# Top-k attention with a routed expert layer: scatters of routed rows right behind the search in the first 66 slots, block pieces from slot 12 of a batch

## The chip, the cores and the metric

The kernel runs on one core of one Trainium2 chip. The metric is the device time of one execution in microseconds (us), and lower is better. Five engines of the core appear in the profile: PE (matrix multiply; PEld is its weight load), DVE (vector), ACT (scalar, activation functions), POOL (GpSimd) and SP (issues DMAs here). Each engine runs its own instructions in the order in which they were written to it, and waits for others through semaphores.

## The reference: what is computed

There are two stages. The first is attention that keeps, for each query, the scores that reach the 32nd largest:

```
scores = scale * (q @ k.T)                  # 8 batches, 8 heads, 576 x 576, head size 64
kth    = 32nd largest of each row
p      = exp(where(scores >= kth, scores, -1e9) - rowmax)
attn   = (p / (sum(p) + 1e-9)) @ v
x      = attn, reshaped to 4608 tokens x 512
```

The second sends each token to one of eight experts:

```
logits = x @ w_gate                         # 4608 x 8
e      = argmax(logits);  gate = softmax(logits)[e]
y      = gate * (relu(x @ w1[e]) @ w2[e])   # w1: 512 x 1024, w2: 1024 x 512
```

All data are 32-bit floats.

## The kernel before, in words

**Slots.** The attention is cut into 144 slots, 18 for each of the 8 batches (`work`, `per_batch`). A slot handles two tiles of 128 queries by 576 keys. The function `loop` (from L1233) writes the instructions slot by slot. In the text slot 25 is the 26th; "slot 2.7" is slot 7 of batch 2, which is slot 43.

**One slot.** In the order in which they are written:

- DVE folds the scores of the *next* slot into halves: larger (`h`, L320) and smaller (`l`, L321). The search of this slot follows (`search`, L358). It works on the larger quarter (`few`) and on short lists of what was set aside (`lists`, L354), and takes eight maxima at a time (MAX8, L379), four times for each tile, with the found ones struck out in between (L390).
- Inside the search `fold_on` (L324) folds `h` of the next slot once more: the larger of each pair into `few` (L327, DVE), the smaller into `hl`. `hl` is made in one of two ways. *Aside*: POOL computes it as a sum of integers less the larger one (L332 and L333). Otherwise DVE takes the minimum (L335). In the aside form `fold_on` stands after the second pass of the search; otherwise it stands before the fourth (after the second too in a "heavy" slot).
- ACT turns the found threshold into `low` (L401) and applies a steep ReLU to the scores (`depths`, L417). POOL subtracts the result from the scores (`less`, L426, twice per slot), so that all below the threshold vanishes in the exponential. POOL also makes `nbias` (L385) and keeps doubts (L407).
- ACT copies later scores out of PSUM (L311). PE transposes the weights of the slot before (L445, L461), does pieces of expert work, and ACT takes the exponential (L434). PE multiplies the scores of the slot four ahead (L304).

**Aside or not.** L1258 to L1260: `loose` holds for slots 1 to 65 (`QUIET = 66`). `soon`, which selects the aside form, holds in a loose slot if `k.crowded` is false. `k.crowded` is set by any scatter, by any store of a finished block and by `rows`. In a slot in which attention rows are scaled by POOL (L519 to L533), the slot is `heavy` and takes the DVE form.

**The end of a batch.** Some slots after a batch's last tile, `ending` (L1111) computes its routing. It is a generator that stops at named places (`yield "small"`, `yield "pool"`); `at_place(name)` in the loop lets it go on. Small DVE operations of it, here called ticks, are handed out one at a time between passes three and four of later searches (`tick`, L339): the choice of the expert (L545 to L558), the places of the tokens (L581 to L590), for the first batch `filled_up` (L696 to L706), and the table of blocks (`table`, L644 to L689). The rows go to `x_rows` in DRAM by five indirect DMAs that POOL issues (`scatter`, L601), one per slot, and only after the fifth are the next blocks' rows and weights loaded (`ahead`, through SP).

**Expert work.** A block is 128 rows of one expert, cut into 16 pieces for PE (eight of the first product, L979, and eight of the second, L996), with ACT evacuating (L870, L984, L1005) and POOL issuing the indirect store (L888). A rate, set anew in slot 13 of each batch (`FIRST`, L1016 and L1286), says how many pieces a slot takes. After the loop the remaining blocks run on PE alone. POOL's order is not written out by hand: what `in_turn` marks keeps its order, and a DMA is only told to stand after the instruction in `k.last_pool` (L606).

Of the kernel before, what the change touches and what calls it, by code (L numbers as in the profile page):

```python
# [12 lines left out]
ALU = mybir.AluOpType  # L13
# [31 lines left out]
def kernel(  # L45
# [47 lines left out]
    nc = tc.nc  # L93
# [40 lines left out]
    k = SimpleNamespace()  # L134
# [122 lines left out]
    def in_turn(put):  # L257

        if not k.exact:
            tc.keep_in_program_order(put)  # L260
        return put
# [62 lines left out]
    def fold_on(f, aside_too=False):  # L324

        f.few = k.att.tile([P, 2, LW], F32, name="few", bufs=3)
        nc.vector.tensor_tensor(f.few[:, :, 0:QF], f.h[:, :, 0:QF], f.h[:, :, QF:HF], op=ALU.max)  # L327
        hl = k.att.tile([P, 2, QF], I32, name="hl", bufs=1)
        f.hl, f.aside = hl[:, :, :].bitcast(F32), aside_too
        if aside_too:  # L330
            one, other, more = (a.bitcast(I32) for a in (f.h[:, :, 0:QF], f.h[:, :, QF:HF], f.few[:, :, 0:QF]))
            in_turn(nc.gpsimd.tensor_tensor(hl, one, other, op=ALU.add))  # L332
            in_turn(nc.gpsimd.tensor_tensor(hl, hl, more, op=ALU.subtract))  # L333
        else:
            nc.vector.tensor_tensor(f.hl, f.h[:, :, 0:QF], f.h[:, :, QF:HF], op=ALU.min)  # L335

# [76 lines left out]
    def depths(s, low):  # L413

        w = k.att.tile([P, 2, S], F32, name="w", bufs=1 if k.exact else 3)
        for m in range(2):
            nc.scalar.activation(  # L417
                w[:, m, :], s[:, m, :, :].rearrange("p j k -> p (j k)"), AF.Relu,
                scale=-STEEP, bias=low[:, m:m + 1],
            )  # L420
        return w
# [591 lines left out]
            evacuate()  # L1013

    PIECES = 2 * FT
    FIRST = 13  # L1016
    ARRIVED = 13
    AHEAD = 3
    QUIET = 66
# [4 lines left out]
    with fast:  # L1024
# [8 lines left out]
        per_batch = len(work) // B  # L1033
        x_of, lg_of = {}, {}
        waiting, loaded, coming, spare, scatters, stores = [], [], [], [], [], []
# [3 lines left out]
        def level(b):  # L1039

            have, sums = left / PIECES, []
            for n, new in enumerate(new_of[b:] + [0], 1):
                sums.append(have / n)
                have += new
            sums[-1] = (have - KEEP / PIECES) / (len(sums) - 1 + (per_batch - FIRST) / per_batch)
            return min(sums)
# [4 lines left out]
        def ahead():  # L1051
            while waiting and len(loaded) < 2:
                expert, piece = waiting.pop(0)
                if isinstance(piece, SimpleNamespace):
                    rows_in = piece
                elif isinstance(piece, list):
                    rows_in = load_half(load_rows(SimpleNamespace(), piece[0]), *piece[1:])
                elif isinstance(piece, tuple):
                    rows_in = load_rows(SimpleNamespace(), *piece, full=True)
                else:  # L1060
                    rows_in = load_rows(SimpleNamespace(), piece)
                loaded.append(load_weights(rows_in, expert))
                loaded[-1].at = clock
# [36 lines left out]
        def scatter(n):  # L1100
            nonlocal left
            for _ in range(min(n, len(scatters))):
                k.crowded = True
                scatters.pop(0)()
            if not scatters and coming:
                waiting.extend(coming)
                left += len(coming) * PIECES
                coming.clear()
                ahead()

        def ending(b, u):  # L1111

            nonlocal left
            n = unit[b * U + u]
            if u == 0:
                x_of[b] = k.xp.tile([P, KC, XW], F32, name="x")
                in_turn(token_ids(x_of[b][:, :, Dm + 1].bitcast(I32), b))
                lg_of[b] = k.small.tile([P, KC, E], F32, name="lg")
            x, lg = x_of[b], lg_of[b]
            out_steps = outputs(n, x)  # L1120
            yield "products"
            next(out_steps)
            yield "relu"
            next(out_steps)
            if u % 2 == 0:
                yield "relu"
            div = divisors(n)
            next(div)
            aside.append(div)
            yield "products"  # L1130
            next(out_steps)
            if b * U + u + 2 < len(units):
                load_values(unit[b * U + u + 2])
            yield "relu"
            next(out_steps)
            yield "products"
            next(out_steps)
            yield "relu"
            next(out_steps, None)
            yield "rows"  # L1140
            through(div)
            logits(n, lg)
            rows(n, x)
            if u < U - 1:
                return
            yield "small"
            r = choice(lg)
            aside.append(r.steps)
            yield "weights"
            yield "turn"  # L1150
            through(r.steps)
            nc.scalar.activation(lg, lg, AF.Exp)
            yield "products"
            ranks(r)
            yield "small"
            steps = places(r, x)
            aside.append(steps)
            yield "relu"
            nc.scalar.copy(run, r.run)
            if b:  # L1160
                nc.scalar.activation(blocks, r.run, AF.Copy, scale=1.0 / P, bias=UNDER)
            yield "pool"
            through(steps)
            scatters.extend(scattering(r, x))
            if b == 0:
                steps = filled_up()
                aside.append(steps)
                yield "weights"
                yield "pool"
                through(steps)  # L1170
            if b == B - 1:
                scatter(KC)
                slot_i = k.small.tile([1, 2, NSLOT], I32, name="slot_i")
                half, full, brief = counted()
                through(table(slot_i, SURE, False, half))
                nc.vector.tensor_scalar_add(done, done, -WHOLE)
                firsts = [(slot_i[0:1, 0, j:j + 1], slot_i[0:1, 1, j:j + 1]) for j in range(SURE)]
                ready = load_rows(SimpleNamespace(), firsts[0][1], True)
            new = LAST - SURE if b == B - 1 else new_of[b]
            if new:  # L1180
                if b == B - 1:
                    slot_i = slot_last
                    steps = end_table(slot_i, slot_long, new, half, full, brief)
                else:
                    slot_i = k.small.tile([1, 2, NSLOT], I32, name="slot_i")
                    steps = table(slot_i, new, False)
                aside.append(steps)
                for _ in range(3 if b < B - 1 else 2):
                    yield "weights"
                    yield "pool"  # L1190
                through(steps)
                coming.extend((slot_i[0:1, 0, j:j + 1], slot_i[0:1, 1, j:j + 1]) for j in range(new))
            if b == B - 1:
                spare.extend(coming[PLAIN:])
                del coming[PLAIN:]
                longs = [[slot_long[0:1, i, j:j + 1] for i in range(3)] for j in range(LONGS)]
                spare.extend((expert, half) for expert, half, _ in longs[HALVES:])
                coming[0:0] = [
                    (expert, [full, half, ST if j >= BRIEF else FEW])
                    for j, (expert, half, full) in enumerate(longs[:HALVES])  # L1200
                ]
                assert len(loaded) == 2
                fill_up()
                coming[0:0] = [(firsts[0][0], ready)] + [(expert, (piece,)) for expert, piece in firsts[1:]]
                scatter(0)
# [3 lines left out]
        def at_place(name):  # L1209
            for end in list(late):  # L1210
                if end[1] == name:
                    end[1] = next(end[0], None)
                    if end[1] is None:
                        late.remove(end)
# [18 lines left out]
        def loop():  # L1233
# [16 lines left out]
            for i, (b, g) in enumerate(work):  # L1250
# [7 lines left out]
                loose = 0 < i < QUIET  # L1258
# [14 lines left out]
                low, nbias, doubts = search(tiles, s_of[i], f_of.pop(i), then, soon, behind, beside)  # L1273
                k.crowded, k.heavy = held, False
                at_place("small")
                w_of[i] = depths(s_of[i], low)
                less(s_of.pop(i), w_of[i])
                doubts()
# [2 lines left out]
                    at_place("relu")  # L1281
                    at_place("rows")
                put_stores()
                scatter(1)
                at = i % per_batch
                if at == FIRST and b:  # L1286
                    rate = level(b) * PIECES / (U * NT)
# [70 lines left out]
    with ExitStack() as outer:  # L1358
        either = nc.values_load(rare_i[0:1, 0:1], min_val=0, max_val=P + 1)  # L1359
        outer.enter_context(tc.If(either > 0))  # L1360
        with ExitStack() as st:
            open_pools(st, True)
            more = nc.values_load(rest_i[0:1, 0:1], min_val=0, max_val=LAST + E)
# [110 lines left out]
```

## Time and profile before

| | |
|---|---|
| time, median of 3 runs | 1282.63 us (1281.47 to 1285.32) |
| time of the profiled execution | 1284.61 us |
| its span | 1283.0 us |
| PE busy | 1176.1 us, 92% of the span |
| DVE busy | 1058.8 us, 83% |
| ACT busy | 933.3 us, 73% |
| POOL busy | 732.0 us, 57% |

Busy times are unions of the instructions' records, so that overlapping records count once. A record of DVE includes time in which the instruction stands in the engine and can't go on. In the stretch of the slots, DVE shows no gaps: what it loses stands inside its records, and shows as a record that is longer than others of the same form. Slot lengths in the text are from the end of the last MAX8 of one slot's search to that of the next one's.

### The profile page before, as it was taken

The numbers are of one execution on the slowest core, as the hardware profiler recorded it, in microseconds if no ns is written. First come the engines' busy times: TensorE is split into PE (matmuls) and PEld (weight loads), VectorE is DVE, ScalarE is ACT, GpSimd is POOL, SyncE is SP. The second block draws the span as 40 slices with busy tenths as digits, with TensorE's granted clock in tenths as the row PEclk, the third lists the DMA queues.
The fourth block names the chain that finished last, engine by engine and source line by source line (L and its number), as shares of the span: only waits on it lengthen the run. The fifth ranks groups of instructions, "written<-read, shape, count | busy, mean of one in ns | idle before, by whom it ended". The sixth has DMA issues, their size and how long they took to land. (4 is left out here: it accounts for less than half of the span.)

```text
span 1283.0 us, 24461 instructions
## 1 busy us (share of the span) xinstructions
PE 1176.1 (92%) x7574; PEld 823.6 (64%) x7574; DVE 1058.8 (83%) x4608; ACT 933.3 (73%) x2136; POOL 732.0 (57%) x884
## 2 busy tenths in 40 slices
PE   6767767898899999999999999999999999999998
PEld 3444444665566566667666666666666667789975
DVE  8999999999999999999999999999999965000000
ACT  4888887988799888888788888888888872112121
POOL 4777777786678665658555855676557743101010
PEclk9888788999899999999999999999999999999999
DMA  5001113741474147533946464547555548996582
GB/s 153 31 30 31 31 39 126 263 157 39 146 251 162 39 150 283 182 135 98 332 142 218 163 224 153 189 146 264 178 178 202 172 149 285 353 358 235 215 301 83
DMA packets 98701, 220.81 MB, mean 172 GB/s; under 512 B 5309, under 2 KB 26301, under 8 KB 98560
## 3 DMA queue, kind: packets, MB, share of 16 engines
q1 hardware_dynamic: 91360, 198.87, 44.5%
q0 software_dynamic: 6384, 19.97, 4.2%
q8 instruction: 61, 1.00, 0.3%
q14 instruction: 80, 0.66, 0.2%
q10 hardware_dynamic: 816, 0.31, 0.1%
HBM read 195.75 MB, written 24.04 MB: 171 GB/s over the span
## 5 line engine op out<-in xcount | busy, mean ns | idle before, releaser
L426 POOL TENSOR_TENSOR w<-s,w 128x576 f32<-128x576 f32 x288 | 409.2, 1441 | 317.5 <-ACT w L417 317.4
L979 PE MATMUL ph<-xTs,w 128*128 128x128 f32 x2112 | 263.0, 278 | 2.6 <-ACT xTs L870 2.6
L979 PEld LDWEIGHTS ph<-xTs,w 128*128 128x128 f32 x2112 | 251.3, 194 | 21.1 <-issue 17.6
L996 PE MATMUL py<-w,hT 128*128 128x512 f32 x528 | 248.7, 600 | 1.9 <-ACT hT L984 1.6
L434 ACT ACTIVATE w<-w,nbias 128x576 f32<-128x576 f32 x288 | 223.0, 785 | 2.3 <-POOL w L426 1.4
L445 PE MATMUL wTm<-turn,w 128*128 128x128 f32 x1152 | 173.9, 291 | 52.7 <-ACT oT L484 29.1
L417 ACT ACTIVATE w<-s,low 128x576 f32<-128x576 f32 x288 | 207.7, 768 | 4.7
L304 PE MATMUL sc<-qkb 64*128 64x288 f32 (+1 forms) x1280 | 200.7, 465 | 7.8 <-DMA qkb<-in_qk_dram 4.0
L445 PEld LDWEIGHTS wTm<-turn,w 128*128 128x128 f32 x1152 | 135.1, 148 | 111.6 <-ACT oT L484 35.5
L311 ACT COPY s<-sc 128x576 f32<-128x576 f32 x288 | 168.0, 634 | 11.9 <-PE sc L304 11.8
L379 DVE MAX8 tops<-scr 128x8 f32<-128x168 f32 x576 | 169.5, 328 | 0.0
L452 ACT COPY wT<-wTm 128x512 f32<-128x512 f32 x256 | 140.7, 596 | 37.8 <-PE wTm L445 37.2
L379 DVE MAX8 tops<-few 128x8 f32<-128x144 f32 (+1 forms) x576 | 154.9, 314 | 0.0
L304 PEld LDWEIGHTS sc<-qkb 64*128 64x128 f32 (+1 forms) x1280 | 107.1, 190 | 71.5 <-issue 35.2
L996 PEld LDWEIGHTS py<-w,hT 128*128 128x128 f32 x528 | 92.0, 191 | 86.5 <-issue 83.0
L482 PE MATMUL po<-wT,vb 128*64 128x288 f32 x1024 | 143.8, 425 | 0.0
L888 POOL DMA_INDIRECT out_dram<-y,xg x37 | 38.9, 1052 | 161.3 <-ACT y L1005 82.0
L356 DVE MAX8 few<-l 128x8 f32<-128x288 f32 x288 | 129.8, 451 | 0.0
L320 DVE TENSOR_TENSOR h<-s 128x576 f32<-128x576 f32 (+1 forms) x145 | 111.7, 770 | 3.9 <-ACT s L311 3.6
L321 DVE TENSOR_TENSOR l<-s 128x576 f32<-128x576 f32 (+1 forms) x145 | 114.3, 788 | 0.0
L482 PEld LDWEIGHTS po<-wT,vb 128*64 128x64 f32 x1024 | 70.1, 141 | 68.9 <-issue 17.4
L356 DVE MAX8 few<-hl 128x8 f32<-128x72 f32 x576 | 102.3, 221 | 0.0
(205 smaller groups left out, 1596.7 us busy)
## 6 DMA issues: line engine op xcount, KB each, us to landing
w<-in_moe_w_dram SPq DMA_DIRECT2D x74, 2048.0 KB, 9.2
qkb<-in_qk_dram SPq DMA_DIRECT2D x31, 608.0 KB, 3.8
vb<-in_v_dram SPq DMA_DIRECT2D x32, 320.0 KB, 3.2
xg<-x_rows SPq DMA_DIRECT2D x37, 257.0 KB, 9.1
x_rows<-blank SPq DMA_DIRECT2D x13, 257.0 KB, 7.9
x_rows<-blank POOLq DMA_DIRECT2D x4, 257.0 KB, 9.8
x_rows<-x,posi POOLq DMA_INDIRECT x40, 3.2
out_dram<-y,xg POOLq DMA_INDIRECT x37, 3.9
```

What stands on the lines that cost most here:

```text
L304: nc.tensor.matmul(ps[rows, j, 0:HF], n.q[d, cols], n.k[d, keys], start=True, stop=True)
L311: lambda m=m, ps=ps: nc.scalar.copy(s[:, m, :, :], ps[:, :, 0:HF]) for m, ps in enumerate(got)
L356: nc.vector.max(out=f.few[:, m, QF + 8 * j:QF + 8 * j + 8], in_=away)
L379: nc.vector.max(out=tops[:, m, r * 8:(r + 1) * 8], in_=src[m])
L417: nc.scalar.activation(w[:, m, :], s[:, m, :, :].rearrange("p j k -> p (j k)"), AF.Relu, scale=-STEEP, bias=low[:, m:m + 1],)
L426: k.last_pool = in_turn(nc.gpsimd.tensor_tensor(w[:, m, :], s[:, m, :, :].rearrange("p j k -> p (j k)"), w[:, m, :], op=ALU.subtract)).ins
L434: nc.scalar.activation(w[:, m, :], w[:, m, :], AF.Exp, scale=scale, bias=nbias[:, m:m + 1], accum_out=n.z[:, c:c + 1])
L445: nc.tensor.transpose(pm[:, c * P:(c + 1) * P], w[:, m, first:first + P], ident)
L452: nc.scalar.copy(wT[:, :, m, q], pm4)
L482: nc.tensor.matmul(po[r, 0:HF], n.v[:, c, r], rhs, start=(c == 0), stop=(c == KC - 1))
L979: nc.tensor.matmul(ph[:, f, :], n.w1[:, 0, dt, fc * P:(fc + 1) * P], n.xT[:, dt, :], start=(dt == 0), stop=(dt == DT - 1),)
L996: nc.tensor.matmul(py, hT[:, f, :], n.w2[:, 0, f, :], start=(f == 0), stop=(f == FT - 1))
```

## The change

There are five edits.

1. In loose slots the scatter moves from the end of the slot's POOL work to right behind the search, ahead of `depths` and `less`.
2. A scatter in a loose slot no longer sets `k.crowded`; in later slots it still does.
3. `fold_on` in its aside form records its second POOL instruction as `k.last_pool`, so that a scatter stands behind it.
4. In the first three batches' endings the places "pool" become "small": the rest of the places and of the table is written right behind the search instead of after `less`.
5. `FIRST` goes from 13 to 12.

```diff
         if aside_too:
...
             in_turn(nc.gpsimd.tensor_tensor(hl, one, other, op=ALU.add))
-            in_turn(nc.gpsimd.tensor_tensor(hl, hl, more, op=ALU.subtract))
+            k.last_pool = in_turn(nc.gpsimd.tensor_tensor(hl, hl, more, op=ALU.subtract)).ins
...
-    FIRST = 13
+    FIRST = 12
...
         def scatter(n):
             nonlocal left
             for _ in range(min(n, len(scatters))):
-                k.crowded = True
                 scatters.pop(0)()
...
-            yield "pool"
+            routed = "small" if b < QUIET // per_batch else "pool"
+            yield routed
             through(steps)
             scatters.extend(scattering(r, x))
             if b == 0:
                 steps = filled_up()
                 aside.append(steps)
                 yield "weights"
-                yield "pool"
+                yield routed
                 through(steps)
...
                 for _ in range(3 if b < B - 1 else 2):
                     yield "weights"
-                    yield "pool"
+                    yield routed
...
                 at_place("small")
+                if loose:
+                    scatter(1)
                 w_of[i] = depths(s_of[i], low)
...
                 put_stores()
-                scatter(1)
+                if not loose:
+                    k.crowded = k.crowded or bool(scatters)
+                    scatter(1)
```

## The prediction, made before the changed kernel ran

> **What bounds the kernel now.** The chain that ended last tells only of the output's last DMAs here, so I first asked for the busy times of three stretches: slots 0 to 65, slots 66 to 143, and the rest. Columns: stretch, its length, then busy time (and count) of PE, PEld, DVE, ACT and POOL, the PE clock, the DMA share, GB/s.
>
> ```profile
> 0.00:472.47 472.47, 384.43 (x2387) 249.25 (x2389) 467.47 (x2057) 394.80 (x909) 342.20 (x428) 0.92 0.31 106
> 472.47:1047.47 575.00, 562.76 (x3775) 387.97 (x3776) 573.09 (x2445) 491.28 (x1137) 358.61 (x420) 1.00 0.55 192
> 1047.47:1283.00 235.53, 228.91 (x1416) 186.34 (x1414) 18.24 (x107) 47.25 (x92) 31.15 (x37) 1.00 0.72 255
> ```
>
> DVE has work or a blocked instruction in all of the slots, so slots last as long as their DVE stream. The last 235.5 us are PE's. In the order of the changed program PE does 383 pieces inside the loop and 513 behind it, exactly as before: the last batch spreads whatever is left. So the tail is the same, and only slot lengths count.
>
> Slot lengths from the DVE timeline: an undisturbed aside slot is 6.55 us (ten of the first 16), an undisturbed one with the DVE form 6.90 (slots 47, 65, 66). So L335 is worth **0.35** (its record is 0.44, 0.1 of it overlapping). A tick adds some 0.08. What is longer than that is blocking. The timelines (start, us, engine, line) show it. Slot 22 is an aside slot with ticks:
>
> ```profile
> 163.35 0.79 POOL L332 TENSOR_TENSOR hl<-h 128x288 int32<-128x288 int32 x1
> 164.22 0.80 POOL L333 TENSOR_TENSOR hl<-hl,few 128x288 int32<-128x288 int32 x1
> ...
> 164.15 0.18 DVE L547 TENSOR_TENSOR lg<-lg,mx 128x40 f32<-128x40 f32 x1
> 164.56 0.52 DVE L549 SCALAR_TENSOR_TENSOR oh<-lg,e_less 128x40 f32<-128x40 f32 x1
> ```
>
> L547 slipped in between two POOL instructions. L549 came during L333 and ended at 165.08, just after it: 0.3 lost. Slot 43 (crowded, DVE form), where `less` of slot 42 is late:
>
> ```profile
> 309.29 2.79 POOL L426 TENSOR_TENSOR w<-s,w 128x576 f32<-128x576 f32 x2 [3.62 <-ACT w L417]
> ...
> 311.27 0.82 DVE L653 TENSOR_SCALAR full<-blocks 1x8 f32<-1x8 f32 x1
> 313.07 0.44 DVE L327 TENSOR_TENSOR few<-h 128x288 f32<-128x288 f32 x1
> 313.44 0.44 DVE L335 TENSOR_TENSOR hl<-h 128x288 f32<-128x288 f32 x1
> ```
>
> A tick on eight numbers took 0.82 (0.14 elsewhere), until L426 was through. And the end of slot 26:
>
> ```profile
> 192.16 1.03 POOL L601 DMA_INDIRECT x_rows<-x,posi  x1 [0.16 <-issue]
> 194.05 1.80 POOL L533 TENSOR_TENSOR x<-xl,rz 128x640 f32<-128x640 f32 x1
> ...
> 194.66 1.81 DVE L321 TENSOR_TENSOR l<-s 128x576 f32<-128x576 f32 x1
> ```
>
> The scatter pushed the row scaling L533 into the folds of slot 27; L321 took 1.81 instead of 0.75. The same stands in slots 45 and 63. Last, POOL's gap in slot 24, into which the scatter is to go:
>
> ```profile
> 178.23 0.79 POOL L333 TENSOR_TENSOR hl<-hl,few 128x288 int32<-128x288 int32 x1
> 181.35 2.79 POOL L426 TENSOR_TENSOR w<-s,w 128x576 f32<-128x576 f32 x2 [2.32 <-ACT w L417]
> ```
>
> **What the skill says.** The Trainium skill, "SBUF — State Buffer", section "Who interferes with whom": a DVE instruction with two SBUF inputs contends with a GpSimd instruction that reads SBUF, whoever issues first has the port for the whole instruction, and tensor_reduce doesn't contend. The trace agrees: L549 and L321 above; reductions (L583, L586) took 0.19 and 0.20 during L333, no more than elsewhere. L581, one input of which is in PSUM, took 0.22 during L332. The same section infers that descriptor generation leaves tensor_tensor alone: nine L327 records under a scatter last 0.435 to 0.441, so a scatter costs POOL 1.04 and DVE nothing. "Perfetto Trace Analysis", section "Optimizing Scalar/DVE Operations", warns that moving work between DVE and GpSimd might not help because of that port; that is the question here.
>
> **The change, part by part.**
>
> *Aside form instead of L335.* By the changed order L335 goes from 13 slots (25, 27, 28, 29; 40, 43, 46, 47, 51; 58, 61, 64, 65) and comes to three (38, 49, 56), where a block's store now falls one slot earlier because of `FIRST`. Net 10 x 0.35 = **-3.5**.
>
> *Scatter in the gap.* L333 ends 0.76 before the slot does, the places' last tick is done 0.2 before it, and L426 starts 1.1 to 1.2 after. A 1.04 scatter with its 0.16 gap fits into 1.9 to 2.3 us. Cover: if it were gone, `less` would start a scatter later, which ACT's exponential and then the next `low` would see. I take **0**.
>
> *New: L332 and L333 under ticks.* Behind an aside L327's end, L332 runs from +0.2 to +1.0 and L333 from +1.07 to +1.87 (slots 24 and 42). Ticks come at +0.76, +1.12, +1.52, then after L333. In slots 27 and 28 the table's ticks come there. In slot 27 L653 loses 0.2 and L659, shifted to 1.34, 0.55: 0.75. In slot 28 the first tick is a reduction (free), the second, L674, arrives at 1.1, just behind L333's start: 0.75. In slot 25 two of `filled_up`'s lose 0.37. In slots 40 and 58 the choice's ticks lose 0.3, as in slot 22. Sum **+2.5**. Bounds: 0.8 if they slip between the two instructions as L547 did, 3.5 if each waits for a whole instruction.
>
> *Slots 43 and 61.* There ACT's `low` of the slot before comes 1.77 late, because PE's second transpose waits for the places' tick L581; the changed order keeps that wait. L426 then runs from +2.86 to +5.65 of slot 43. In the aside form L327 asks at +3.94, not +6.65: it waits some 0.3 for the first half and gets in before the second; L653 then loses 0.6, as it does now; and L332 and L333, now at +6.4 to +8.1, lie on L659 to L670 for another 0.4 to 0.5. **+0.75** each, +1.5 for both; bounds 0.3 to 1.9 each, the upper if L327 waits for both halves.
>
> *L327 against a late `less` elsewhere.* The aside slot's L327 comes at +3.94 and an undisturbed `less` ends at +3.95. If `low` is late by t, L327 loses t - 0.2 (late 0.67 before slot 34: 0.46 lost; 0.60 before 17: 0.38). In the DVE form at +5.6 it loses nothing up to t = 1.7. Slot 25 (late 0.47): 0.26. Slots 40 and 58 (late 1.44 and 0.58 now, and I take 0.6): 0.4 each. Slots 47 and 65, behind a slot in which ACT evacuates both an attention product and L984: 0.44 each. Sum **+1.9**, bounds 0.5 and 4.
>
> *Relief.* L984 and L870 leave ACT's slots 40 and 58, so L327 of slots 42 and 60 no longer loses 0.44 and 0.37. In slots 44 and 62 a store and a scatter now both stand ahead of L519: L533 falls behind the folds into the MAX8 part, so that the 1.05 on L321 goes, while a later `less` costs a tick about half of that and the small L519 some more: -0.3 each. In slot 26 one scatter stands ahead of L519 as before, and the 1.05 stays. Sum **-1.4**, bounds -3 and 0.
>
> *Table and loads.* The last scatter of batch 0 was issued at 214.27 and landed at 217.28; rows and weights were issued at 217.43 to 218.59, the first weights landed at 226.15. In the changed order the first block's transposes come in slot 30 instead of 31, some 6.9 us earlier, at about 227.5; the scatter is some 4 us earlier within its slot. Landed in time, cost 0; if the loads weren't earlier, the margin would be 1.3.
>
> *`FIRST`.* PE is ahead by 2 pieces from slot 30 to about slot 105, behind by 1 to 3 after it, and even at the end. That changes which slots hold an L870, an L984 or a store, and so which L327 meets a late `less`. Such losses over 0.25 add up to 33 us in this execution. The same evacuations fall on other slots: I take **0** and +-3.
>
> Sum: -3.5 + 2.5 + 1.5 + 1.9 - 1.4 = **+1.0** on the profiled execution's 1284.6. Against the median, which is 2.0 below that, **1283.6**. Changes under 0.3% (3.85 us) are about what a measurement of this kernel can't tell from none.
>
> **The rivals.** *(a) The saving stays whole.* Ticks slip between POOL's instructions, as L547 did, and slots 43 and 61 lose only what they lose now: -3.5 - 1.4 = -4.9, so 1277.7. For it: ten undisturbed aside slots, none of them with such ticks. Against it: slot 22, aside with ticks, took 7.69 (0.26 of it at L320, behind slot 21's row scaling) where slot 40 with as many ticks and the DVE form took 7.54.
>
> *(b) Slower: L327 waits for all of a late `less`* in slots 40, 43, 58 and 61. This decides once `low` lags by more than about 1.1, since then L426's second half still blocks at +3.94 and L332 and L333 start where the slot should end. Price up to 1.4 each, 5.6, less the 1.4 taken for L327 in these four already (0.4 + 0.3, twice): +4.2 more, 1287.8. For it: 1.77 before slots 43 and 61 by construction, 1.44 before slot 40. Against it: in slot 139 L327 came during the first half and got in between the halves.
>
> *(c) The earlier pieces shorten the run,* since PE is only 81% busy up to slot 65 (384.43 of 472.47). Two pieces are at most 2 us of PE, and the loop ends with the same 383 done while DVE sets the slots: 0. Nothing beyond the sum, 1283.6.
>
> **How the numbers follow.** My sum (and (c), which gives the same time) 0.62; (a), with a favourable shuffle of the late evacuations, 0.22; (b), with an unfavourable one, 0.16. Faster than 1278.8 is what (a) gives, slower than 1286.5 what (b) gives: 0.22, 0.62, 0.16. The terms' bounds don't all fall on one side; with the +-3 of the shuffle some 5 to each side hold 8 in 10, reaching to both rivals: 1277.5 to 1288.5.
>
> **What would show it.** L335 x97 instead of x107. Right: records of L653, L659, L674 or L700 well over 0.14 to 0.2 in slots 25, 27, 28, 43 and 61, ending when L332, L333 or L426 end; L601 in POOL's gap ahead of L426, with L426 still 1.1 to 1.2 behind the slot's end; slot 27 no shorter than 8.4; pieces from slot 30; a stretch behind the loop of 235 us. Wrong: slots 25 to 29 shorter by 1.4 in sum with normal ticks, which means (a); slots 43 and 61 above 9.2, which means (b); a tail of another length, or PE waiting for weights in slot 30, which none of this holds.

## The result and the profile after

The changed kernel took 1292.44 us, median of 6 runs (1291.26 to 1292.86), the kernel before beside it 1285.01 (6 runs): a ratio of 1.0059, 95% interval 1.0049 to 1.0070. A second set gave 1293.57 against 1284.66, 1.0068 (1.0054 to 1.0083). So the change costs some 7 to 9 us, where the prediction had 1283.6 us and a range up to 1288.5.

The first profiled execution took 1291.26 us (span 1289.6). Its busy times in the three stretches (slots 0 to 65, slots 66 to 143, the rest), with the same columns as before:

```profile
0.00:477.24 477.24, 388.06 (x2387) 249.34 (x2387) 472.37 (x2047) 395.31 (x911) 358.42 (x448) 0.93 0.30 104
477.24:1052.18 574.94, 559.81 (x3769) 387.23 (x3768) 574.08 (x2445) 489.62 (x1132) 353.09 (x420) 0.99 0.55 192
1052.18:1289.65 237.47, 230.80 (x1422) 187.20 (x1419) 18.27 (x108) 48.73 (x95) 31.17 (x37) 0.99 0.73 256
```

The first stretch is 4.8 us longer and the last, which was to stay at 235, 1.9. DVE ran ten instructions fewer in the first and was busier all the same (472.37 us against 467.47): what it lost stands inside its records. The groups of DVE's costliest lines (busy us, mean ns of one, idle before) show where:

```profile
L321 DVE TENSOR_TENSOR l<-s 128x576 f32<-128x576 f32 (+1 forms) x145 | 111.1, 766 | 0.0
...
L327 DVE TENSOR_TENSOR few<-h 128x288 f32<-128x288 f32 x144 | 84.4, 586 | 0.0
...
L335 DVE TENSOR_TENSOR hl<-h 128x288 f32<-128x288 f32 x97 | 48.6, 501 | 0.0
```

L335 fell from 107 to 97, as predicted. L321 lost 3.2 us of blocking (114.3 before), L327 gained 4.2 (80.2 before). By stage, with the second profile of the same kernel beside the first (us, change against before):

| slots | before | after | after, second profile |
|---|---|---|---|
| 0 to 24 (same code) | 179.79 | +1.43 | +0.15 |
| 25 to 29 | 37.16 | +0.67 | +0.71 |
| 30 to 32 | 20.30 | 0.0 | 0.0 |
| 33 to 35 | 20.56 | +3.00 | +2.54 |
| 36 to 47 | 86.01 | -0.76 | -0.68 |
| 48 to 51 | 28.81 | -1.26 | -0.31 |
| 52 and 53 | 13.86 | +2.20 | +2.78 |
| 54 to 65 | 85.96 | -0.51 | +0.07 |
| 66 to 143 | 575.00 | -0.05 | +0.71 |
| behind the loop | 235.54 | +1.92 | +1.99 |

Slots 33 to 35, 52 and 53 and the tail carry the loss. The timeline of the changed kernel (start, us, engine, line) shows steps that were predicted, L321 behind the row scaling and ticks under L332 and L333. Its first line, a scatter of 1.74 us where 1.04 was taken, and its last two were not predicted:

```profile
181.32 1.74 POOL L601 DMA_INDIRECT x_rows<-x,posi  x1 [0.86 <-DVE tops L379]
183.09 2.79 POOL L426 TENSOR_TENSOR w<-s,w 128x576 f32<-128x576 f32 x2
185.24 0.96 DVE L327 TENSOR_TENSOR few<-h 128x288 f32<-128x288 f32 x1
...
195.94 1.80 POOL L533 TENSOR_TENSOR x<-xl,rz 128x640 f32<-128x640 f32 x1
196.55 1.81 DVE L321 TENSOR_TENSOR l<-s 128x576 f32<-128x576 f32 x1
...
201.65 0.78 POOL L332 TENSOR_TENSOR hl<-h 128x288 int32<-128x288 int32 x1
202.19 0.26 DVE L653 TENSOR_SCALAR full<-blocks 1x8 f32<-1x8 f32 x1
202.51 0.79 POOL L333 TENSOR_TENSOR hl<-hl,few 128x288 int32<-128x288 int32 x1
202.62 0.69 DVE L659 TENSOR_TENSOR left<-full,done 1x8 f32<-1x8 f32 x1
...
210.23 0.80 POOL L333 TENSOR_TENSOR hl<-hl,few 128x288 int32<-128x288 int32 x1
210.26 0.79 DVE L674 SCALAR_TENSOR_TENSOR slot_f<-slot_f,done,slots_less 1x3 f32<-1x3 f32 x1
...
249.96 2.77 POOL L426 TENSOR_TENSOR w<-s,w 128x576 f32<-128x576 f32 x2 [1.64 <-ACT w L417]
...
251.58 1.48 DVE L327 TENSOR_TENSOR few<-h 128x288 f32<-128x288 f32 x1
```

L659 and L674, eight and three numbers, last until L333 is through, and slot 27 keeps the 1.05 us that L321 loses to the row scaling. In slot 34 (from 246.75) ACT's `low` was 2.1 us late, so `less` starts at +3.2 instead of +1.1, and L327 loses 1.0.

### The profile page after: what moved, and what is told of

It reads as the page before. It is cut to its first block, busy times and chain, and to the rows that moved or that the text cites. A ratio compares the mean times of both kernels' runs of the same rounds, so it can differ in the third digit from the quotient of the medians.

```text
span 1289.6 us, 24498 instructions
## 1 busy us (share of the span) xinstructions
PE 1178.7 (91%) x7574; PEld 823.8 (64%) x7574; DVE 1064.7 (83%) x4598; ACT 933.7 (72%) x2136; POOL 742.7 (58%) x904
## 5 line engine op out<-in xcount | busy, mean ns | idle before, releaser
L979 PE MATMUL ph<-xTs,w 128*128 128x128 f32 x2112 | 262.3, 278 | 2.6 <-ACT xTs L870 2.6
L979 PEld LDWEIGHTS ph<-xTs,w 128*128 128x128 f32 x2112 | 249.9, 193 | 22.2 <-issue 18.8
L445 PE MATMUL wTm<-turn,w 128*128 128x128 f32 x1152 | 171.3, 288 | 52.1 <-ACT oT L484 27.2
L482 PE MATMUL po<-wT,vb 128*64 128x288 f32 x1024 | 148.4, 435 | 0.0
L320 DVE TENSOR_TENSOR h<-s 128x576 f32<-128x576 f32 (+1 forms) x145 | 109.4, 755 | 3.9 <-ACT s L311 3.5
L321 DVE TENSOR_TENSOR l<-s 128x576 f32<-128x576 f32 (+1 forms) x145 | 111.1, 766 | 0.0
```

Of the source, the lines that this page charges most:

```text
L445: nc.tensor.transpose(pm[:, c * P:(c + 1) * P], w[:, m, first:first + P], ident)
L482: nc.tensor.matmul(po[r, 0:HF], n.v[:, c, r], rhs, start=(c == 0), stop=(c == KC - 1))
L979: nc.tensor.matmul(ph[:, f, :], n.w1[:, 0, dt, fc * P:(fc + 1) * P], n.xT[:, dt, :], start=(dt == 0), stop=(dt == DT - 1),)
```

## The experiments

All ratios are to the kernel before, run beside it. Slot lengths are each from one profile. Three profiles below hold the same instructions up to slot 65 (the run "Ticks without the aside form" and the two with `FIRST` at 12 from batch 3 on), and these slots took 469.2, 473.0 and 476.4 us. So a difference of a few us between two profiles is not by itself one of the code; it needs a second profile, or a look at the clock and the scatters in both.

**The changed kernel again.** No edit.

> The changed kernel once more, unaltered, to see which of the slot lengths of its first profile belong to the kernel. Medians so far: 1285.0 us before, 1292.4 after. If the lost time is the program's own, slots 33 to 35 come out longer than before by 3.0 us in sum again, slots 52 and 53 by 2.2, and the stretch behind the loop is 237.5 us again instead of 235.5. If it is one execution's accident, these differ by more than 1 us from the first profile. For slots 0 to 24, whose code is the same in both kernels and which were 1.4 us longer after, I expect the accident: they come out within 1 us of before.

1293.57 us. The table above has the slots: 33 to 35, 52 and 53 and the tail come out long again, slots 0 to 24 within 0.15 of before. So 1.3 us of the first profile's front was an accident, and the rest is the program's.

**The two halves of the change.** The first run is the changed kernel with

```diff
-    FIRST = 12
+    FIRST = 13
```

> FIRST back at 13, the four edits on scatters, k.last_pool and places kept. Theory P (the phase of the block pieces costs): slots 33 to 35, 52 and 53 and the tail go back to their lengths before, and what is left is the scatter part, which by the slots is worth between -1.5 and +1; time 1284 to 1286.5 us. Theory S (a scatter in POOL's gap puts less, and so the exponential and the next low, late): the loss stays, 1290 to 1293 us, and slots 33 to 35 still hold L327 records over 1 us. Also expected: slots 25, 27 and 28 as in the changed kernel (7.7, 8.7 and 8.2 us or so), since FIRST does not touch them.

and the second the kernel before with `FIRST` at 12.

> The kernel before with FIRST at 12 and nothing else. Theory P: slots 33 to 35 grow by 2 to 3 us in sum, with ACT's low 1 us or more late ahead of each and L327 blocked; slots 48 to 53 shift both ways; the tail becomes 237 us; time 1289 to 1292 us. Theory S: no change, 1285 us, and no late low ahead of slots 33 to 35.

The scatter part alone: 1285.93 us (22 runs), ratio 1.0012 (1.0004 to 1.0019). `FIRST` alone: 1291.47, ratio 1.0055 (1.0042 to 1.0068). The two add up to the whole, and theory S falls: `FIRST` carries 6.8 of some 8 us. By its profile, `FIRST` alone adds 1.4 us in slots 33 to 35, 2.8 in slots 52 and 53, 1.8 in slots 66 to 143 and 1.9 behind the loop; the rest gets 1.1 shorter. One thing did not go as theory P had it: with `FIRST` back at 13, slots 33 to 35 are still 1.1 us longer than before. The timeline of slot 32 shows why. This is the scatter part alone (the first three lines are of slot 27, for the last section):

```profile
193.55 0.73 DVE L320 TENSOR_TENSOR h<-s 128x576 f32<-128x576 f32 x1
193.59 1.81 POOL L533 TENSOR_TENSOR x<-xl,rz 128x640 f32<-128x640 f32 x1
194.20 1.81 DVE L321 TENSOR_TENSOR l<-s 128x576 f32<-128x576 f32 x1
...
235.39 3.60 PE L979 MATMUL ph<-xTs,w 128*128 128x128 f32 x16 [0.62 <-ACT xTs L870]
238.92 1.24 PE L304 MATMUL sc<-qkb 64*128 64x288 f32 x8
...
240.19 1.18 ACT L311 COPY s<-sc 128x576 f32<-128x576 f32 x2 [1.49 <-PE sc L304]
...
465.39 2.33 POOL L601 DMA_INDIRECT x_rows<-x,posi  x1 [0.17 <-issue]
467.75 2.78 POOL L426 TENSOR_TENSOR w<-s,w 128x576 f32<-128x576 f32 x2
469.82 2.13 DVE L327 TENSOR_TENSOR few<-h 128x288 f32<-128x288 f32 x1
```

Sixteen L979 took 3.60 us, because PE's granted clock was at half for 3.4 us from 4.8 us into slot 32 on. In the next run, which has the same pieces there, they took 2.05:

```profile
234.39 2.05 PE L979 MATMUL ph<-xTs,w 128*128 128x128 f32 x16 [0.62 <-ACT xTs L870]
236.37 1.24 PE L304 MATMUL sc<-qkb 64*128 64x288 f32 x8
```

The scores came 1.5 us later, ACT waited 1.49 for them, `low` was 2.2 late after slot 33, and DVE paid. The changed kernel has such a stretch too, from 5.0 us into slot 31 on, and `FIRST` alone has none between 2.8 us into slot 31 and slot 41. So of the 2.5 to 3.0 us that the changed kernel loses in slots 33 to 35, 1.4 goes with the pieces alone, and the rest stands beside a stretch of half clock. (The last three lines of the longer timeline are a scatter that took 2.33 us to issue: `less` came 1.05 late, and L327 lost 1.7 in slot 65, for POOL's L332 got in ahead of it as well.)

**Ticks without the aside form.** As the scatter part alone, with

```diff
-                soon = loose and (k.heavy or not k.crowded)
+                soon = loose and (k.heavy or not (k.crowded or i in (25, 27, 28, 43, 61)))
```

> As the kernel with the scatter part alone, and slots 25, 27, 28, 43 and 61, in which L332 and L333 fell on ticks, take the DVE form (five L335 more). By the prediction's terms the aside form costs 1.0 more there than it saves in 25, 27 and 28 (0.37 + 0.26, 0.75, 0.75 against 3 times 0.35 is +1.1) and 0.75 less 0.35 in each of 43 and 61: some 1.9 us in sum, so it should be 1.5 to 2 us faster than the kernel with the scatter part alone. The rival, that ticks slip between POOL's instructions for nothing: five L335 more cost 1.75, so it is slower by that.

1283.20 us (14 runs), 2.7 below the scatter part alone; ratio 0.9992 (0.9981 to 1.0002). The rival falls: five L335 more, and faster. By the slots: 25 and 28 give back 0.41 and 0.23, 43 and 61 0.41 each. Slot 27 gives back 1.12, more than its ticks cost, since L321 is not blocked at all in this run; a later run, with slot 27 alone, puts its ticks at 0.33. So the ticks come to 1.8, as expected, and L321 adds 0.8. The two profiles also differ where the edit changes nothing: slot 65's scatter (2.0 less) and slots 33 to 35 (1.1 less), slots 0 to 24 (0.7 more) and everything from slot 66 on (2.2 more).

**Whose are slots 33 to 53?** The changed kernel with the pieces of before in slots 30 to 53:

```diff
+                if 30 <= i < 54:
+                    now = PLAN[i - 30]
```

> The changed kernel, whole, but in slots 30 to 53 each slot takes as many block pieces as in the kernel before (0, 4, 1, 3, 4, 1 in slots 30 to 35, 1, 5, 1, 3, 5, 0 in slots 48 to 53); the two or three pieces that are then missing come in slots 54 to 57. Theory Q (the count of pieces by slot is what makes ACT's low late there, since a sixth piece in slots 31 and 49 and a fourth in 33 and 51 put PE's transposes and L984 in front of it): slots 33 to 35 and 52 and 53 lose what they had gained in length, 2.5 and 2.8 us in sum, slots 48 to 51 give back 0.3; slots 66 on stay as in the changed kernel; so 4.5 to 5 us below the changed kernel's 1293.1: 1288 to 1289 us. The rival, that FIRST costs through the time at which rows and weights are loaded or through the lower rate after slot 66 alone: 1292 us or more, with slots 33 to 35 still at 23 us in sum.

1291.12 us, ratio 1.0050, and not the 1288 to 1289 expected. Slots 52 and 53 came to 13.83: all of their loss is back, so theory Q holds there. Slots 33 to 35 came to 21.77, which is what the scatter part alone has, with the same stretch of half clock 5.0 us into slot 32. But slots 54 to 65 grew from 86.0 to 88.4: the pieces left over landed in slots 55 and 56 (7 and 3), and `low` was 2.3 to 2.6 late ahead of slots 57 and 58 (8.84 and 8.72 us). The loss moved with the pieces.

**Is it the place of L327?** The changed kernel with `i in (34, 35, 52, 53)` in the same condition as above.

> The changed kernel, but slots 34, 35, 52 and 53 take the DVE form, so that L327 comes at about +5.6 us of the slot instead of +3.95. The plan of pieces stays, and ACT's low stays as late as it is (1 to 2.6 us). Theory R (a late low costs only because L327 of the aside form meets POOL's less): the L327 excesses of 1.0, 0.77, 1.1 and 0.77 us go, four L335 come back at 0.35 each; 8.46 becomes 7.5 to 7.8, 7.70 becomes 6.92, 8.93 becomes 7.9, 7.71 becomes 6.92, so 3 us in sum, 1290 us. Rival: DVE itself waits for ACT or PE there (for s of a later slot), and the slots stay within 0.4 us of 8.46, 7.70, 8.93 and 7.71, the wait standing in another instruction.

1293.70 us: no gain. Slots 35 and 53 are heavy and have the DVE form anyway, so only 34 and 52 changed. They fell to 7.80 and 8.22 (7.5 to 7.8 and 7.9 were expected); but 35 and 53 grew from 7.70 and 7.71 to 8.23 and 8.26, where L335 now lost 1.2. The pairs are 16.03 and 16.48 us against 16.16 and 16.64 in the second profile of the changed kernel. Theory R falls for these slots: what DVE doesn't wait for in one slot it waits for in the next. This fits a lag of PE and ACT that only shows in DVE's stall.

**Which piece?** The changed kernel in slots 49 to 53 shows the chain. In this timeline slot 50 starts at 362.25, 51 at 369.10 and 52 at 375.73:

```profile
366.17 0.40 ACT L484 COPY oT<-po 128x288 f32<-128x288 f32 x1 [0.69 <-PE po L482]
...
370.10 0.60 ACT L984 ACTIVATE hT<-ph 128x512 f32<-128x512 f32 x1 [0.53 <-PE ph L979]
370.59 0.20 ACT L401 ACTIVATE low<-tops 128x2 f32<-128x2 f32 x1
371.67 3.10 POOL L426 TENSOR_TENSOR w<-s,w 128x576 f32<-128x576 f32 x2 [2.85 <-ACT w L417]
...
378.84 2.78 POOL L426 TENSOR_TENSOR w<-s,w 128x576 f32<-128x576 f32 x2 [1.52 <-ACT w L417]
...
380.56 1.37 DVE L327 TENSOR_TENSOR few<-h 128x288 f32<-128x288 f32 x1
```

ACT waits for PE twice, with L984 in front of L401; `low` is 1.5 and 2.0 late after slots 50 and 51, and L327 of slot 52 pays 0.9 (L321 0.6 more). Three runs moved single pieces. Two from slots 49 and 51 to 50 (`now += {49: -1, 50: 1}.get(i, 0)`, and the carry moves the other):

> The changed kernel, with one block piece moved from slot 49 to slot 50; the carry then moves a second one from 51 to 50, so that slots 49 to 52 take 5, 2, 3, 4 pieces instead of 6, 0, 4, 4. If the sixth piece in slot 49 is what puts PE's oT product and with it ACT's low late (3.0 us after slot 50, 2.6 after slot 51), both lags fall under 1.5 us and slots 50 to 53, 31.0 us in the second profile of the changed kernel, come to 29 us or less. If it is the place of the three evacuations (oT, hT, xT still stand together in slot 51), slots 52 and 53 stay at 16 us or more.

One from 51 to 52:

> The changed kernel, with one block piece moved from slot 51 to slot 52, so that slots 49 to 52 take 6, 0, 3, 6 pieces instead of 6, 0, 4, 4. If the sixth piece in slot 49 is the cause, the lag of low after slot 50 stays at 3 us, and slots 50 to 53 stay within 1 us of 31.0. If the fourth piece in slot 51 is the cause, slots 52 and 53 fall from 16.6 to 14.5 us or less.

One from 49 to 50 alone:

> The changed kernel, with the sixth piece of slot 49 moved to slot 50 and nothing else: slots 49 to 53 take 5, 1, 4, 4, 0 pieces instead of 6, 0, 4, 4, 0. The run that moved two pieces was disturbed by a half-clock stretch of PE in slot 48. If the sixth piece is the cause, low lags by less than 2 us after slots 50 and 51 (3.0 and 2.6 in the changed kernel), and slots 52 and 53 come from 16.6 to 15 us or less. If the sixth piece is not the cause, they stay at 16.6 within 0.4.

The times were 1293.85 and 1291.56 (one run each) and 1292.37 (ratio 1.0059). In the second, slots 52 and 53 were 16.63 beside 16.64 in a profile with the same clock: the fourth piece of slot 51 is not it. The first had stretches of half clock from slots 46 and 50 on, with lengths of 7.97 and 7.67 in 48 and 49, and missed its 29 us (30.1). But the last run below, which has the changed kernel's pieces there, had the same stretches and the same lengths in 48 to 51; its slots 52 and 53 took 16.64, and these 15.25. So about half of the 2.8 us goes with the moved pieces. In the third, 52 and 53 fell to 14.08, as expected; but a slow scatter (2.33 us) had made slot 47 1.35 us longer, which may have let PE catch up. Slots 47 to 53 took 49.6 us in all, against 50.2 in the first profile of the changed kernel, which has no half clock there either, and 51.7 in the second, which has some in slot 49. A sixth piece in slot 49 is part of the cause. How large a part these runs do not settle.

**A piece count later, and only late.** On the kernel without the aside form in the tick slots, `FIRST` at 14, and `FIRST` at 12 from batch 3 on:

> The same kernel with FIRST at 14 throughout: the first pieces come a slot later instead of a slot earlier. If an earlier start costs by itself, a later one gains: 1278 to 1281 us. If FIRST is a phase, which puts five or six pieces and ACT's evacuations on one or another slot of a batch, either sign is possible; by the order of the instructions slots 33 and 51 take five pieces here and hold oT and hT copies (three and oT alone before, four and all three in the changed kernel), so I expect a late low ahead of slots 34 and 52 and 1283 to 1288 us.

> The kernel without the aside form in the tick slots (1283.2 us), with FIRST at 12 from batch 3 on only; so slots up to 65 keep the pieces of before. If the phase also costs behind slot 66, the stretch from slot 66 to the end is 2 to 4 us longer (it was 810.6 in the kernel before, 812.4 to 814.3 in the three kernels with FIRST 12) and the time is 1285 to 1287. If FIRST costs only in slots 33 to 53, it stays at 1283 within 0.7. The tail should be longer by some 2 us here too, since slots 141 and 142 take 12 pieces where before they took 10.

`FIRST` at 14: 1290.53 us, ratio 1.0043 (1.0026 to 1.0059), 7.3 above the same kernel with 13. So a later start does not gain, and an earlier one does not cost by being earlier. The places that I named, 34 and 52, are not longer; 33, 35 and 53 are, by 0.6, 0.8 and 0.5. But the pieces of 13 show as much where the clock or a scatter is the same as here: with a half-clock stretch 3.3 us into slot 31, slots 33 to 35 took 21.47 here and 21.96 in the next run, and behind a slow scatter in slot 46, slot 53 took 7.45 here and 7.87 in the repeat below. So in sum, up to slot 65, this run shows no loss that the pieces of 13 don't show too. The largest part, 5 us, lies behind slot 66, and its cause was not tried. `FIRST` at 12 from batch 3 on was expected to lose 2 to 4 us and gained: 1281.76, ratio 0.9967 (0.9953 to 0.9981). The tail grew to 238.2, as expected, but slots 66 to 143 fell to 569.4. The repeat:

> The scatter part with the DVE form in the five tick slots and FIRST 12 from batch 3 on, unaltered from its first run, to settle whether it beats the kernel before: 1281 to 1282.5 us, ratio 0.997 with an upper end below 1. If the first result came from a few lucky executions (two of eight were at 1278), the ratio comes out at 0.999 or above.

1281.12 us (21 runs) against 1284.31, ratio 0.9971 (0.9961 to 0.9980). It beats the kernel before by some 3 us, and with it the changed one. Against the same kernel with 13 throughout the gain is 1.5 to 3 us, compared across sets.

These runs also separate the clock from the code, because up to slot 65 two of them hold the same instructions. Busy times of slots 31 and 32 and of slots 33 to 35, first of the run with `FIRST` at 13 throughout:

```profile
222.63:236.00 13.37, 8.87 (x68) 6.03 (x65) 13.37 (x60) 12.07 (x29) 10.26 (x13) 1.00 1.04 397
236.00:256.56 20.56, 20.06 (x148) 15.09 (x149) 20.56 (x90) 19.30 (x46) 15.62 (x20) 1.00 0.36 114
```

and then of the first run with 12 from batch 3 on:

```profile
224.35:237.71 13.36, 10.45 (x56) 5.91 (x52) 13.36 (x60) 10.79 (x25) 10.29 (x13) 0.74 1.04 397
237.71:259.67 21.96, 21.46 (x160) 16.48 (x161) 21.96 (x90) 20.66 (x50) 15.44 (x20) 1.00 0.36 115
```

The PE clock (third figure from the end) was 1.00 in one and 0.74 in the other, and the three slots behind it took 20.56 and 21.96. The Trainium skill, "TensorE: Matmul & The Clock Gate", Part 1, says that the clock is at full or half rate, decided in windows of 3413 ns that run on regardless of the kernel. The traces agree: the stretches of half clock last 3.41, 6.83 or 10.24 us (17.07 or 20.48 at the front of five profiles), all whole multiples of 3.413, except the one that the end of each profile cuts off. Where they fall decides 1.4 us here.

**Slot 27 alone.** The scatter part alone with `i == 27` in the condition.

> The scatter part alone, FIRST at 13, with the DVE form put back in slot 27 only. Slot 27 should fall from 8.70 to 7.6 us, 25 and 28 stay at 7.83 and 7.71. In five profiles with the aside form there, slots 33 to 35 were 1.1 us longer than with the same pieces and the DVE form, and a stretch of half PE clock 10.2 us long began 8 us into slot 27, with another in slot 32 on the 16 products L979 (3.60 us instead of 2.05). If the long slot 27 brings that, the first half-clock stretch is 3.4 us and slots 33 to 35 come to 20.6 us. If the aside form in 25 and 28 brings it, they stay at 21.7.

1284.11 us (one run). The positions in that expectation were read on a zero 10.6 us off: the long stretch begins 4.2 us into slot 26, the other 4.8 us into slot 32. Slot 27 came to 8.37 instead of 7.6: its ticks are worth 0.33, and L321 still loses 1.06. The long stretch did fall to 3.4 us, but slots 33 to 35 stayed at 21.77, because a half-clock stretch lay on slot 32 all the same. Since slot 27 stayed long, this run alone does not clear it. Two others do: in the kernel before slot 27 took 8.36 and slots 33 to 35 took 20.56, and in the first run with 12 from batch 3 on 7.57 and 21.96. So slot 27's length does not decide it, and what does stays open.

**Behind slot 66.** The changed kernel with the pieces of before, slot by slot, from slot 66 on:

> The changed kernel, with its own pieces up to slot 65 and those of the kernel before, slot by slot, from 66 on (both have done 96 by then and 383 at the end of the loop). If the counts by slot decide that stretch too, slot 66 to the end takes 809 to 811 us, as in the kernels with FIRST 13 (810.6, 808.9, 811.1), and not 812.4 to 814.3; the tail is 235.8 us and not 237.5; the time falls from 1293 to 1290 or 1291. If the stretch was long because of what happened earlier or of the loads' times, it stays at 813.

1292.61 us, ratio 1.0065, and not 1290 or 1291. The tail went back to 236.15, and slots 106 to 143 to 278.2 (275.7 in the changed kernel, 278.1 before): these two are a matter of where the last pieces stand. But slots 66 to the end took 812.3 us, not 809 to 811. The four profiles with `FIRST` at 13 have 808.9 to 811.1, the changed kernel 812.4 and 813.2. So the counts by slot bring back the tail but next to nothing in sum, and what makes slots 66 on longer with `FIRST` at 12 stays open.

## Why the prediction was wrong

**The failed step** is the one headed `FIRST`: "The same evacuations fall on other slots: I take 0 and +-3." By itself it measured 6.8 us. Two things were wrong in it. It took a change of phase as a draw of mean zero. What the runs show is a lag that goes with the pieces: with those of before, slots 52 and 53 lost all of their 2.8 us, and where the left-over pieces went, slots 57 and 58 grew by 1.9 and 1.2 against the kernel before. A sixth piece in slots 31 and 49, with four more two slots on, is more than what was there before (four and five, then three). That the lag builds up because PE and ACT together get more than a slot's length of work is my reading of the timelines, and not shown apart. The other thing is PE's room. The step doesn't ask for it, and rival (c) reads it off an average, 81% busy up to slot 65. Slots 33 to 35 of the kernel before and of the changed one:

```profile
237.26:257.82 20.56, 20.07 (x148) 15.09 (x149) 20.56 (x90) 19.30 (x46) 15.60 (x20) 1.00 0.55 193
239.36:262.92 23.56, 22.30 (x151) 15.45 (x151) 23.40 (x90) 20.84 (x50) 15.82 (x20) 1.00 0.46 160
```

PE was busy 20.07 of 20.56 us there before the change. It had half a microsecond of room in three slots. Of the 6.8 us, slots 33 to 35, 52 and 53 hold 4.1 and the tail 1.9, with 1.1 less elsewhere; the 1.8 in slots 66 to 143 have no cause that a run shows, and there 12 from batch 3 on even gained.

**The tail** was "the same, and only slot lengths count", since both orders do 383 pieces in the loop. That count is right, but slots 141 and 142 take 12 of them instead of 10, and PE is not through with them when DVE ends: 1422 matmuls behind DVE's last MAX8 instead of 1416, and 1.9 us.

**The slots whose form or ticks change** were right, most within 0.15 us. Change of length against before, from the prediction's terms with the 0.35 for L335 put in, in the scatter part alone, and in the whole:

| slot | predicted | scatter part alone | changed kernel |
|---|---|---|---|
| 25 / 27 / 28 / 29 | +0.28 / +0.40 / +0.40 / -0.35 | +0.44 / +0.34 / +0.24 / -0.35 | +0.44 / +0.32 / +0.25 / -0.36 |
| 43 / 61 | +0.40 / +0.40 | +0.44 / +0.43 | +0.43 / +0.43 |
| 40 / 58 (form changes with `FIRST` only) | +0.35 / +0.35 | 0.0 / 0.0 | +0.40 / +0.40 |
| 42 / 60 | -0.44 / -0.37 | 0.0 / -0.37 | -0.44 / -0.36 |
| 45 / 63 | -0.30 / -0.30 | 0.0 / 0.0 | -0.68 / -0.68 |
| 46 / 64 | -0.35 / -0.35 | -0.35 / -0.35 | -0.36 / -0.36 |
| 47 / 65 | +0.09 / +0.09 | -0.35 / +1.65 | -0.35 / -0.18 |

Together with the slots to which L335 moves or from which it goes (51: -0.37; 38, 49, 56: +0.37, +0.54, +0.36) they sum to -0.2 in this profile of the changed kernel and to +1.4 in its second one (slots 51 and 61 make the difference), where +1.0 was forecast. The scatter part alone was measured at +1.3 (0.5 to 2.4 by its interval), so its total would have fitted the forecast. That is in part luck: in its profile slot 65's slow scatter (+1.65) and the half clock before slots 33 to 35 (+1.1), neither of them forecast, stand against 1.9 less in slots 66 to 143. *(a)*, the saving stays whole, is out: slots 25 to 29 grew by 0.7. *(b)*, L327 waits for all of a late `less` in 40, 43, 58 and 61, is out for 43, which took 8.46 to 8.48 and not over 9.2, and for 61 in most profiles (8.47 here). But slot 61 took 9.15 in the second profile of the changed kernel and 9.10 in the run with the late form, close to (b). The mechanism of (b) did strike, but in slots 34, 35, 52 and 53, for which `FIRST` made `low` late.

**The scatter in POOL's gap**, taken at 0, holds when it takes 1.04 us. The first of a batch took 1.57 to 1.74 there, in every profile with it, the third of batches 1 and 2 (slots 45 and 63) 1.90 and 1.92 in the changed kernel, and one in slot 64 of the scatter part alone 2.33. What that costs, in L327 of an aside slot, is the cover that the step named and did not price: 0.5 in slot 25 (0.26 forecast) and 1.7 in slot 65.

## What to carry to other kernels

Where an even share of filler work is dealt out in whole pieces, its phase is a parameter with a price of its own: 12 and 14 each cost about 7 us against 13, while 12 from batch 3 on gained 1.5 to 3. Read the room for it slot by slot, on every engine that the piece passes through, and not from an engine's mean load; and do not change it along with something else. When an engine seems to stall at one instruction, look whether moving that instruction helps or only moves the stall: here DVE stalled at L327 because ACT's `low` and POOL's `less` came late, and postponing L327 in two slots gained nothing. And before a difference between two profiles is put to the code, look whether identical code shows it too.

## What the runs showed of the hardware

**A tie for the shared port.** In slot 27 POOL's L533 and DVE's L320 and L321 meet. The timeline of the kernel before with `FIRST` at 12:

```profile
193.40 0.73 DVE L320 TENSOR_TENSOR h<-s 128x576 f32<-128x576 f32 x1
193.43 2.49 POOL L533 TENSOR_TENSOR x<-xl,rz 128x640 f32<-128x640 f32 x1
194.05 0.74 DVE L321 TENSOR_TENSOR l<-s 128x576 f32<-128x576 f32 x1
```

In the scatter part alone (above) L533 took 1.81 and L321 1.81. In both L533 waits for L320. Then either L533 goes and L321 waits for it, or L321 goes as well and L533 waits for two. In slot 27 of the sixteen profiles, POOL went first where L533's record began 45 to 66 ns behind L320's (eleven), and DVE where it began 2 to 33 ns behind (five). There is no fixed limit: in other slots L533 lost at 47 and 52 ns and won at 38. Where its record began 61 to 68 ns ahead of L320's, it still waited for both (2.60 us); at 123 to 315 ahead it went at once (1.25 to 1.26) and L320 waited (it took 1.55 to 1.75). The slot's length hangs on the tie by 0.8 us (8.37 in the run with slot 27 alone, 7.58 in the one without the aside form, both with the DVE form there). The Trainium skill, "SBUF — State Buffer", section "Who interferes with whom", says that the order of issue decides who blocks; here, in slot 27, some ten nanoseconds separate the two outcomes, and the earlier start of POOL was the losing one. So the start of a record does not tell who was granted the port. So a term like "the 1.05 stays" can flip from an edit elsewhere.

**An indirect DMA's issue has a tail.** The 40 of a run take 1.04 us on POOL in the median, but in each of the sixteen profiles one to ten took 1.4 to 2.3. Why was not tried.
